# Three small extra reads early in an attention block with adaptive layer norm

## The chip, the cores and the metric

The kernel runs on one core of one Trainium2 chip. A core has five engines that run side by side: TensorE (PE, matrix products), VectorE (DVE), ScalarE (ACT), GpSimd (POOL) and SyncE (SP, which here only issues DMAs). Sixteen DMA engines move data between the chip's main memory and the core's on-chip memory. The metric is the device time of one execution in microseconds (us).

## The reference

It is one attention block of a diffusion transformer. Inputs in bf16: x is 2 x 256 x 1152, c is 2 x 1152, wqkv is 1152 x 3456, wo is 1152 x 1152, w_mod is 1152 x 6912.

```
mod = (silu(c) @ w_mod) in six parts of D: shift, scale, gate, and three that are not used
h   = layernorm(x) * (1 + scale) + shift
q, k, v = h @ wqkv in three parts
p   = softmax(q @ k.T * D**-0.5)          per batch
out = x + gate * ((p @ v) @ wo)
```

## The kernel before

All 512 tokens (2 batches of 256) are held on chip as four tiles of 128 rows, x_sb[0] to x_sb[3]; tiles 0 and 1 are the first batch, 2 and 3 the second. D = 1152 is nine blocks of 128 (k = 0 to 8). The weights come in once, each in pieces.

The start works against the loads. Thirteen matmuls on constants (the fillers) keep TensorE busy until x arrives. Statistics of the layer norm are taken from x tiles 1 and 0, the tiles are centred, turned by TensorE (tp) and copied into xnT. Meanwhile silu(c) is formed from c_sb and, times the pieces of wS (the scale part of w_mod), gives the scale of the first three blocks (scale_A, psS and psSA). VectorE multiplies xnT by the scale into hTs, and TensorE starts on k = h @ wK while the rest is still loading: k_part(0), k_part(1) and k_part(2) over the first batch with row blocks 0, 1 and 2 of wK into six accumulators (acc) and early_half into psE; then x tile 3, x tile 2 and the other row blocks. After that come the shift part (wH), q (wqv pieces 0 to 2), the scores, softmax, v, attention, and the product with wo, gated and added to x.

The order on each engine is written out: every instruction made through vec, sca, ten, spq or gps is recorded, and pin() chains each record in that order. Nearly all DMAs go out on SyncE's queue through spq, in this order: x tiles 1, 0, 3; five pieces of wS (the first three blocks' columns, row pairs 0-2, 2-4, 4-6, 6-8, 8-9); row block 0 of wK in two parts (wK0); row block 1 (wK1); x tile 2; row block 2 (wK2); then further wS and wK pieces, wH, wqv, wG, wO. ScalarE's queue issues c_sb at the start (line 130) and one output piece at the end. These two are called on nc.scalar itself, so pin() does not chain them.

The framework gives each DMA the next of eight completion semaphores in turn, over both queues together. A DMA that takes a semaphore waits until its holder before, eight places earlier, has landed. In the built program of before, the places are: x1, x0, c, x3, then the wS pieces. So wS's fifth piece waits for x1, wK0's parts for x0 and c, wK1 for x3, x2 for wS's first piece, and so on.

Most instructions bear line 74 in the profile, the line of the recording helper, so groups are told by their tiles.

Of the kernel before, what the change touches and what calls it, by code (L numbers as in the profile page):

```python
# [11 lines left out]
BF16 = mybir.dt.bfloat16  # L12
# [4 lines left out]
def kernel(  # L17
# [9 lines left out]
    nc = tc.nc  # L27
    P = 128
    B, N, D = x.shape
# [16 lines left out]
    x_f = x.rearrange("b n d -> (b n) d")  # L46
# [5 lines left out]
    const = ctx.enter_context(tc.tile_pool(name="const", bufs=1))  # L52
# [43 lines left out]
    def tok(b):  # L96
# [5 lines left out]
        out=ident, in_=ident, compare_op=ALU.not_equal, fill=1.0, base=0,  # L102
# [14 lines left out]
        out=pick, in_=pick, compare_op=ALU.is_ge, fill=0.0, base=0,  # L117
# [3 lines left out]
        out=pick, in_=pick, compare_op=ALU.is_ge, fill=0.0, base=NT - 1,  # L121
# [6 lines left out]
    x_sb = act.tile([P, TT, D], BF16)  # L128
    nc.scalar.preload_act_table_set("natural_log_exp_and_others")
    nc.scalar.dma_start(out=c_sb, in_=c.rearrange("b (p k) -> p b k", p=P))  # L130

    wK = wpool.tile([P, KT, D], BF16)
    chunk_cols = [vc * CW for vc in range(NCH)] + [2 * D + vc * CW for vc in range(NCH)]
# [580 lines left out]
```

## Time and profile before

| what | value |
|---|---|
| median of 3 runs | 98.16 us (97.86 to 98.18) |
| profiled execution | 97.95 us, of which 96.2 us span |
| TensorE clock granted, mean | 0.996 |
| DMA moved | 21.31 MB, 222 GB/s over the span |
| x_sb loads, 288 KB each | issue to landing 2.8 / 3.8 / 4.5 us (least, median, most) |
| c_sb load, 4.5 KB | issue to landing 2.9 us |

The span runs from the first to the last instruction; the rest of the execution's time lies around it. A wait in the profile is put down to the releaser that came last. "Landing" is when a DMA's completion semaphore has its full count. A line of the chain of waits gives start, length and the work that held the end up. TensorE's busy time is modelled at the ends of matmuls, so starts are the firmer numbers. SPq and ACTq are the times in which SyncE and ScalarE issue DMAs.

### The profile page before, as it was taken

How to read it: one execution, taken by the hardware profiler on the slowest of the kernel's cores; microseconds unless marked ns; L12 is line 12 of the kernel's file. 1: busy time of each engine (PE TensorE's matmuls, PEld its weight loads, DVE VectorE, ACT ScalarE, POOL GpSimd, SP SyncE). 2: the span in 40 equal slices, each digit the busy share in tenths (PEclk: the TensorE clock that was granted, in tenths of full speed). 3: DMA queues.
4: the chain of work that ended last, by engine and by line, in shares of the span. 5: the costliest groups of instructions: out<-in, count | busy, mean ns of one | idle time of the engine just before them, and what ended most of it. 6: DMA issues, size and time to landing. Idle time of an engine off the chain costs nothing.

```text
span 96.2 us, 1804 instructions
## 1 busy us (share of the span) xinstructions
PE 91.2 (95%) x715; PEld 55.5 (58%) x720; DVE 70.6 (73%) x139; ACT 33.5 (35%) x67; POOL 21.4 (22%) x26
## 2 busy tenths in 40 slices
PE   5998899999999999999999999999999999999970
PEld 1338698454566444444458755665568755665760
DVE  0488589132999999999982999990229577999880
ACT  5297667202560962432231445331115400000010
POOL 6600000710000000000000000008999980007000
PEclk9999999999999999999999999999999999999998
DMA  2999999999999999999999502200000000303221
GB/s 47 303 350 344 348 391 375 396 395 407 395 380 400 383 407 393 373 371 372 383 410 410 220 2 55 50 5 0 0 0 0 7 0 0 123 1 122 98 97 51
DMA packets 19015, 21.31 MB, mean 222 GB/s; under 512 B 2752, under 2 KB 13632, under 8 KB 19008
## 3 DMA queue, kind: packets, MB, share of 16 engines
q1 hardware_dynamic: 18592, 21.16, 61.4%
q10 hardware_dynamic: 416, 0.05, 0.4%
q8 instruction: 5, 0.08, 0.3%
q14 instruction: 2, 0.02, 0.0%
HBM read 19.76 MB, written 1.18 MB: 218 GB/s over the span
## 4 chain that ended last, share of the span: by engine, by line
PE 85%; DMA 9%; DVE 1%; SPq 1%; issue 1%; ACT 0%
PE ps L74 63%; PE acc L74 12%; DMA x_sb<-in_x_dram 4%; DMA wK<-in_wqkv_dram 4%; PE s_ps L74 4%; PE psH L74 2%; PE psE L74 1%; PE tp L74 1%; SPq L74 1%; PE psL L74 1%; DVE xnT L74 0%; PE spread_ps L74 0%; ACT o_sb L74 0%; DVE hTs L74 0%; DVE o_sb L74 0%
## 5 line engine op out<-in xcount | busy, mean ns | idle before, releaser
L74 POOL PARTITION_ALL_REDUCE gate_bc<-gacc x2 | 13.7, 6886 | 45.5 <-DVE gacc L74 45.5
L74 DVE SCALAR_TENSOR_TENSOR gacc<-wG,scT_f,gacc 128x1152 f32<-128x1152 bf16 x16 | 22.7, 1418 | 0.5
L74 PE MATMUL ps<-wqv,hT 128*128 128x384 bf16 x108 | 17.7, 326 | 0.0
L74 PE MATMUL ps<-hT,wqv 128*128 128x512 bf16 x80 | 17.6, 379 | 0.1
L74 PE MATMUL ps<-wO,attnT 128*128 128x384 bf16 (+1 forms) x108 | 17.0, 319 | 0.0
L74 PEld LDWEIGHTS <-attnT 128*128 128x128 bf16 x117 | 11.3, 98 | 6.3
L74 PEld LDWEIGHTS <-hT 128*128 128x128 bf16 x108 | 10.6, 98 | 6.9
L74 PE MATMUL acc<-hTs,wK 128*128 128x128 bf16 (+2 forms) x88 | 13.3, 292 | 0.8 <-DVE hTs L74 0.3
L74 PEld LDWEIGHTS <-wK 128*128 128x128 bf16 x123 | 9.9, 97 | 6.5 <-DMA wK<-in_wqkv_dram 0.7
L74 PEld LDWEIGHTS <-wqv 128*128 128x128 bf16 x81 | 7.8, 97 | 9.6 <-DVE hT L74 0.4
L74 ACT CAST qkT<-ps 128x512 bf16<-128x512 f32 x10 | 5.8, 583 | 10.9 <-PE ps L74 10.9
L74 DVE TENSOR_TENSOR ga<-ps,gate_bc 128x384 f32<-128x384 f32 (+1 forms) x12 | 6.5, 538 | 2.4 <-PE ps L74 2.4
L74 ACT CAST v_sb<-ps 128x384 bf16<-128x384 f32 x10 | 4.7, 476 | 9.8 <-PE ps L74 9.8
L74 DVE TENSOR_TENSOR o_sb<-ga,x_sb 128x384 bf16<-128x384 f32 (+1 forms) x12 | 7.0, 585 | 0.4
L74 DVE TENSOR_TENSOR xnT<-xnT,rstd_bc 128x512 bf16<-128x512 bf16 x9 | 5.5, 685 | 1.8 <-ACT rstd_bc L74 1.8
L74 PE MATMUL junk_ps<-junk_rhs 128*128 128x512 bf16 x13 | 5.7, 627 | 1.1 <-DVE junk_rhs L74 1.1
L74 ACT CAST o_sb<-ps 128x128 bf16<-128x128 f32 x1 | 0.3, 265 | 17.3 <-PE ps L74 17.3
L74 DVE BATCH_NORM_STATS2 stats<-x_sb 128x6 f32<-128x384 bf16 x6 | 3.1, 552 | 2.5 <-DMA x_sb<-in_x_dram 2.5
L74 PE MATMUL ps<-hTs,wK 128*128 128x512 bf16 x19 | 4.7, 378 | 0.1
L74 DVE CAST attnT<-ps 128x512 bf16<-128x512 f32 (+1 forms) x6 | 3.5, 603 | 1.7 <-PE ps L74 1.7
L74 DVE COPY xnT<-tp 128x384 bf16<-128x384 bf16 (+2 forms) x7 | 2.2, 347 | 3.3 <-PE tp L74 3.3
L74 DVE CAST v_sb<-ps 128x384 bf16<-128x384 f32 x2 | 1.1, 558 | 4.6 <-PE ps L74 4.6
(84 smaller groups left out, 91.8 us busy)
## 6 DMA issues: line engine op xcount, KB each, us to landing
wqv<-in_wqkv_dram SPq DMA_DIRECT2D x5, 864.0 KB, 10.1
wG<-in_w_mod_dram SPq DMA_DIRECT2D x3, 864.0 KB, 9.6
wO<-in_wo_dram SPq DMA_DIRECT2D x3, 864.0 KB, 8.5
wH<-in_w_mod_dram SPq DMA_DIRECT2D x4, 576.0 KB, 7.8
wS<-in_w_mod_dram SPq DMA_DIRECT2D x6, 288.0 KB, 6.0
wK<-in_wqkv_dram SPq DMA_DIRECT2D x6, 288.0 KB, 6.2
x_sb<-in_x_dram SPq DMA_DIRECT2D x4, 288.0 KB, 3.8
wqv<-in_wqkv_dram SPq DMA_DIRECT2D x3, 288.0 KB, 9.0
```

Source lines behind the costliest of these rows:

```text
L74: r = fn(*a, **k)
```

## The change

Behind the load of c, ScalarE's queue issues three more reads into a new tile, seen, of 16 partitions. The first takes the first 16 elements (32 bytes) of every eighth row of x tile 2 (16 rows), the second the same of x tile 3. The third takes 32 bytes at column D of every eighth row of wqkv's first 384 rows, 48 rows. Nothing reads seen. The instructions of the other engines keep their order; the three reads take three places in the rotation of the completion semaphores, between x3 and the first piece of wS, so all later DMAs stand three semaphores further.

```diff
     nc.scalar.dma_start(out=c_sb, in_=c.rearrange("b (p k) -> p b k", p=P))
+
+
+    seen = const.tile([16, 5, 16], BF16)
+    for i in range(2):
+        nc.scalar.dma_start(out=seen[:, i, :], in_=x_f[2 * P + i * P : 3 * P + i * P : 8, 0:16])
+    nc.scalar.dma_start(
+        out=seen[:, 2:5, :], in_=wqkv[0 : 3 * P, D : D + 16].rearrange("(k e r) n -> e k r n", k=3, r=8)[:, :, 0, :])
 
     wK = wpool.tile([P, KT, D], BF16)
```

## The prediction

> **What bounds the kernel now.** I read the busy shares first, then the chain that ended last by line, then the same chain in order of time over the first 16 us, then TensorE's timeline, SyncE's timeline and waits, and the DMA rates by stretch.
>
> ```profile
> PE 91.2 (95%) x715; PEld 55.5 (58%) x720; DVE 70.6 (73%) x139; ACT 33.5 (35%) x67; POOL 21.4 (22%) x26
> PE 85%; DMA 9%; DVE 1%; SPq 1%; issue 1%; ACT 0%
> ```
>
> TensorE is the bound, and 85% of the chain lies on it. The 9% of DMA, some 8.7 us, must all lie early. The chain in order of time shows where:
>
> ```profile
> 0.79 0.40 SPq L74
> 1.25 0.41 SPq L74
> 1.71 4.33 DMA x_sb<-in_x_dram
> 6.05 4.32 DMA wK<-in_wqkv_dram
> 10.41 0.83 PE acc L74 x6
> 11.24 0.45 PE tp L74 x8
> 11.69 0.22 PE psE L74 x2
> ```
>
> The reader is to see a chain with two links of DMA. The third load of x (x3, rows 384 to 511, issued at 1.71) lands at 6.03. Only then does SyncE issue the load of wK's second row block (wK1, 256 KB), which lands at 10.37, and TensorE starts on it at 10.41. From there to the end the chain is almost pure TensorE. A change in the first 10 us can therefore move the end by what it moves that start at 10.41, no more in the good direction than the wait there, and one for one in the bad direction.
>
> ```profile
> 9.09 0.81 PE L74 MATMUL acc<-hTs,wK 128*128 128x256 bf16 x6 [0.33 <-DVE hTs L74]
> 9.74 0.38 PE L74 MATMUL psE<-hTs,wK 128*128 128x256 bf16 x2
> 10.41 0.83 PE L74 MATMUL acc<-hTs,wK 128*128 128x256 bf16 x6 [0.29 <-DMA wK<-in_wqkv_dram]
> 11.78 0.83 PE L74 MATMUL acc<-hTs,wK 128*128 128x256 bf16 x6
> ```
>
> The two psE matmuls begin at 9.74. The chain counts such a pair as 0.22 us of work, so TensorE could have gone on at 9.96 and stood until 10.41: 0.45 us (0.29 by the modelled ends). That is the whole prize of an earlier wK1. The wait at 9.09 is for VectorE's hTs, which waited for scale matmuls that follow each other closely from 8.20; an earlier DMA does not shorten it.
>
> ```profile
> 2.17 2.48 SPq L74 DMA_DIRECT2D wS<-in_w_mod_dram  x5
> 4.70 1.68 SPq L74 DMA_DIRECT2D wK<-in_wqkv_dram  x3
> SPq L74 <- DMA x_sb<-in_x_dram: 0.4, 1, 0.4
> ```
>
> SyncE issues about every 0.5 us (5 in 2.48) and its one wait for an x load, 0.4 us, stands ahead of wK1. The rates by stretch, columns as busy time of PE, PEld, DVE, ACT and POOL, then TensorE's clock, the share of the DMA engines and GB/s, say why x3 and wK1 were late:
>
> ```profile
> 2.50:3.50 1.00, 1.00 (x4) 0.31 (x3) 0.00 (x0) 0.00 (x0) 0.86 (x3) 1.00 1.05 341
> 3.50:4.50 1.00, 1.00 (x4) 0.31 (x3) 0.87 (x3) 0.23 (x2) 0.58 (x1) 1.00 0.91 254
> 5.50:8.00 2.50, 2.50 (x33) 1.39 (x31) 2.10 (x6) 2.29 (x7) 0.00 (x0) 1.00 1.09 368
> 8.00:10.00 2.00, 1.67 (x30) 1.42 (x27) 1.68 (x9) 1.60 (x2) 0.00 (x0) 1.00 1.01 333
> ```
>
> The transfers dip to 254 GB/s while x3 comes in and to 333 while wK1 and the last x load (x2, rows 256 to 383) come in; between, they run at 368. In the trace's packets these dips are single packets: most 2304-byte packets take 93 ns, but eight started between 3.63 and 4.07 take 250 to 1027 ns, and six of 2048 or 2304 bytes between 8.03 and 9.47 take 382 to 1289. The extra reads go to just these rows: x's second batch and wqkv's first 384 rows.
>
> **The change part by part.** It removes nothing.
>
> Three more issues on ScalarE's queue, behind that of c. One takes 0.46 us (c's row), so they end near 1.27 + 3 x 0.5 = 2.8. ScalarE's first work waits for c until 3.76. Cost nothing; the cover is 0.9 us of that wait. Without it, the 0.22 us e_sb would come later, then VectorE's silu and ScalarE's copy scT_rep, which itself stands behind act_mean(0) until 5.88.
>
> The bytes themselves: 80 rows of 32 bytes. c's read is the like: its queue shows 272 packets in the stretch 2.0 to 4.5 at a share of 6.1% of 16 engines, 0.15 us per engine. The three reads make 80 data packets and about as many completions as three c's (48): 128/272 x 0.15 = 0.07 us per engine, if nothing in them is slow. They wait behind c's packets (first at 2.5) and pass between x0's and x3's. If each met what x3 met, an engine would stand 0.25 to 1.0 us instead. Lower bound 0.07, upper 1.0; I take 0.1, nearest to c, since c's own packets also read rows nobody had read and took under 0.19.
>
> SyncE's order of waits, the largest part, which the diff does not tell. Each DMA takes the next of eight completion semaphores in turn, and a DMA waits until the one eight places before it has landed. In the built program the three reads take places 4 to 6. So these move forward to an earlier partner's wait: wS's second piece waited for nothing and now waits for x1 (landed 3.56), the third for x0 (4.46), the fourth for c (3.74), the fifth for x3 (6.03; before, for x1). wK0's two parts and wK1 wait for the extra reads, already landed by then. Issue times: second piece 2.65 to 3.58; third 3.16 to 4.48; fourth 3.67 to 4.98; fifth 4.18 to 6.05; wK0's parts 4.69 and 5.17 to 6.55 and 7.05; wK1 6.05 to 7.55; x2 6.61 to 8.05; wK2 7.13 to 8.55. SyncE no longer has wK1 directly behind x3's landing, but three issues later: 1.5 us.
>
> Is that covered? wK1 needed 4.32 us from issue to landing, most of it spent behind earlier transfers. The quickest landing in the trace of a load of that size is x1's, 2.8 us for 288 KB on an empty queue; an output of 288 KB took 2.1. With 7.55 + 2.8 = 10.35 it lands exactly when it did; with 2.1, at 9.65, the queue and not the issue decides and nothing moves; with the full 4.32, at 11.87, 1.5 us late. The engines that are ahead run dry for up to 0.8 us (8.0 us of work begun at 8.6), so the lead that absorbs the next slow packet is gone: if the slow packets of wK1 stay, the engine that meets one ends later by part of that. Between 0 and 1.5 I take 0.25, nearest to x1's row. The scale pieces have less room (kk 8 runs at 8.52, its fifth piece landed at 8.46), but 6.05 + 1.6, the time of a 72 KB output on an empty queue, is 7.65, so the backlog still decides there; only the 0.1 us of extra packets passes through.
>
> By the Trainium skill, DMA: Bandwidth & Descriptors, section Latency and other measured facts, an HBM access takes 0.2 us on average and 2 us at high load. By that rule the slow packets come from load, and reading their rows ahead cures nothing; by the opposite, that they are the first access to something, the sum would be -0.45 + 0.1. No run here shows yet which holds.
>
> What the trace says of it: wK0's parts are the first reads of wqkv and come between 6.2 and 8.0 with no slow packet; the wS pieces first touch w_mod's rows over its whole length with at most 259 ns; and at 11.3 two 768-byte packets take 446 and 341 ns in rows whose neighbours had been read. First contact alone does not make a packet slow here. So I take the slow packets as staying.
>
> Sum: +0.1 (packets) + 0.25 (wK1 issued later) = +0.35 us at 10.41. Behind it TensorE stands only some 0.2 us (at 15.02, for hTs), so nothing gives it back. The profiled execution took 97.95, 96.2 of it span; 98.3 is its sum. The median of the runs shown is 0.21 higher, so against it the forecast is 98.5.
>
> **The rivals.** (1) The reads do cure x3, x2 and wK1. Then x3 lands near 5.3 (x1 and x0 landed 0.9 apart), wK1 is issued at 6.8 and lands by 9.9, and the wait at 10.41 goes: -0.45 + 0.1 = -0.35, 97.8. For it: the slow packets sit in exactly those rows. Against it: wqkv's and w_mod's first reads, and the short lead, since the reads' packets come about 3.3 and x3's from 3.63. It decides once wK1 lands before 10.2. Next late would be wK2 (landed 11.73, used at 11.78), which must come 0.4 earlier too. (2) All is covered: the backlog hides the later issues, 98.2. For it: 2.1 us for an output. Against it: the 0.8 us of dry engines. (3) The reads meet slow packets themselves and hold all engines ahead of x3 and the scale pieces: 0.6 to 1.0 us, of which nothing is covered since kk 8 has 0.06 us to spare: 98.9 to 99.1. Against it: c's packets.
>
> **How the numbers follow.** Forecast case 0.45, 98.5 with its own range 98.2 to 98.9; cure 0.31, 97.7 to 97.9; covered 0.12, 98.1 to 98.3; early hold 0.12. A measurement of this kernel tells 0.3% (0.3 us) from no change. Faster: 0.28 of the cure. Same: 0.03 of the cure, 0.12 covered, 0.15 of the forecast case (its lower third), 0.30. Slower: 0.30 + 0.12 = 0.42. The range has to hold the cure and most of the early hold: 97.6 to 99.0.
>
> **What would show it.** In the profile after: the scale pieces issued in a row with gaps from 3.6 on; SyncE's wait for x_sb ahead of the fifth scale piece; wK1 issued near 7.5 and landing 10.4 to 11; the wait for wK at TensorE larger than 0.29; the rate still dipping between 3.5 and 4.5 and 8 and 10. The prediction is wrong if those dips are gone, if the wait for wK is gone, or if wK1 lands as early as before although issued 1.5 us later.

## The result and the profile after

The changed kernel takes 100.78 us (median of 4 runs, 100.43 to 101.28) against 98.06 us before (97.86 to 98.18, 4 runs): a ratio of 1.0289, 95% interval 1.0243 to 1.0334. It is slower by 2.7 us. The prediction had the direction, but 98.5 us and a range that ended at 99.0. Where an execution below ran at a lower granted clock (0.983, three in all), the medians count it and the ratios do not.

The profiled execution took 100.82 us, 98.9 us of it span. Its busy shares and the chain by engine:

```profile
PE 91.5 (93%) x715; PEld 55.4 (56%) x720; DVE 70.6 (71%) x139; ACT 33.5 (34%) x67; POOL 21.8 (22%) x26
PE 64%; DMA 21%; SPq 10%; issue 1%; ACT 0%; DVE 0%
```

TensorE does the same work in 91.5 us, but its share of the chain fell from 85% to 64%. DMA went from 9% to 21%, and SyncE's issuing (SPq), which had 1%, now has 10%. The chain in order of time (start, length, what held the end up) shows where:

```profile
1.25 3.32 DMA x_sb<-in_x_dram
4.59 0.37 SPq L74
5.00 0.47 SPq L74
5.51 0.47 SPq L74
...
7.92 5.17 DMA wK<-in_wqkv_dram
13.14 0.83 PE acc L74 x6
...
29.69 3.56 SPq L74
33.30 0.85 SPq L74
34.19 12.43 DMA wqv<-in_wqkv_dram
46.66 6.00 PE ps L74 x27
```

Before, the chain from 31 us on has TensorE alone here:

```profile
31.01 10.74 PE ps L74 x49
41.80 8.37 PE ps L74 x38
```

There are two losses, not one. The first is where I looked: x0's landing at 4.57 lets SyncE issue the third scale piece, then seven more follow at about 0.47 us each, and the load at their end, wK2, lets TensorE go on at 13.14. The matmuls that began at 11.78 before begin 1.36 us later. TensorE's starts show how the delay grows from load to load:

```profile
9.62 0.49 PE L74 MATMUL acc<-hTs,wK 128*128 128x256 bf16 x3 [0.33 <-DVE hTs L74]
10.82 0.50 PE L74 MATMUL acc<-hTs,wK 128*128 128x256 bf16 x3 [0.71 <-DMA wK<-in_wqkv_dram]
11.49 0.83 PE L74 MATMUL acc<-hTs,wK 128*128 128x256 bf16 x6
13.14 0.83 PE L74 MATMUL acc<-hTs,wK 128*128 128x256 bf16 x6 [0.15 <-DMA wK<-in_wqkv_dram]
```

The matmuls on wK0 begin 0.53 us late (9.62 for 9.09, behind the scale pieces) and stand again for wK0's second part; those on wK1 are 1.08 us late (11.49 for 10.41) and those on wK2 1.36.

The second loss is paid at 46.66, where TensorE stands for a wqv load. Before, it never waited there. SyncE's long issues of large loads around 30 us are not new: the one that takes 3.56 us took 3.35 before. The waits of TensorE that a DMA or VectorE ended in the changed kernel, a part of the list:

```profile
PE acc L74 <- DMA wK<-in_wqkv_dram: 0.9, 2, 0.7
PE ps L74 <- DMA wqv<-in_wqkv_dram: 0.7, 1, 0.7
PE tp L74 <- DVE xc L74: 0.5, 1, 0.5
PE psS L74 <- DMA wS<-in_w_mod_dram: 0.3, 1, 0.3
```

The DMA rates by stretch (columns as in the prediction's table, the last one GB/s) carry the rest. In the kernel before:

```profile
5.00:10.00 5.00, 4.67 (x60) 3.03 (x58) 4.29 (x15) 4.39 (x9) 0.00 (x0) 1.00 1.05 351
30.00:48.00 18.00, 17.89 (x109) 8.41 (x107) 17.64 (x26) 7.62 (x14) 0.00 (x0) 1.00 1.07 384
```

In the changed kernel:

```profile
5.00:10.00 5.00, 3.81 (x55) 2.56 (x53) 3.91 (x13) 4.66 (x9) 0.00 (x0) 1.00 0.88 258
30.00:48.00 18.00, 17.20 (x117) 8.11 (x116) 15.32 (x25) 7.04 (x13) 0.00 (x0) 1.00 1.08 351
```

Early the engines run dry: share 0.88, 258 GB/s instead of 351. Between 30 and 48 us the DMA engines are as busy as before (1.08 and 1.07), so they have work enough, and yet they move 351 GB/s instead of 384. Three reads of 2.5 KB in all, over by 6 us, cannot do that directly. In the packets of that stretch a row of 768 bytes takes 40.6 ns on average instead of 36.0 and one of 2304 bytes 100.4 instead of 93.6. Nothing in the prediction covers that.

### The profile page after: what moved, and what is told of

Its sections match the earlier page's. It is cut to its first block, busy times and chain, and to the rows that moved or that the text cites. A ratio compares the mean times of both kernels' runs of the same rounds, so it can differ in the third digit from the quotient of the medians.

```text
span 98.9 us, 1807 instructions
## 1 busy us (share of the span) xinstructions
PE 91.5 (93%) x715; PEld 55.4 (56%) x720; DVE 70.6 (71%) x139; ACT 33.5 (34%) x67; POOL 21.8 (22%) x26
## 4 chain that ended last, share of the span: by engine, by line
PE 64%; DMA 21%; SPq 10%; issue 1%; ACT 0%; DVE 0%
PE ps L74 46%; DMA wqv<-in_wqkv_dram 13%; PE acc L74 11%; SPq L74 10%; DMA wK<-in_wqkv_dram 5%; PE s_ps L74 4%; DMA x_sb<-in_x_dram 3%; PE psE L74 1%; PE psM L74 1%; PE psL L74 1%; PE tp L74 1%; PE spread_ps L74 0%; ACT o_sb L74 0%; DVE o_sb L74 0%; PE turn_ps L74 0%
## 5 line engine op out<-in xcount | busy, mean ns | idle before, releaser
L74 PE MATMUL junk_ps<-junk_rhs 128*128 128x512 bf16 x13 | 4.9, 561 | 1.1 <-DVE junk_rhs L74 1.1
L74 ACT ACTIVATE xc<-x_sb 128x1152 bf16<-128x1152 bf16 x3 | 3.5, 1161 | 2.7 <-DMA x_sb<-in_x_dram 2.7
```

Of the source, the lines that this page charges most:

```text
L74: r = fn(*a, **k)
```

## The experiments

The first theory was SyncE's waits (the places among the eight completion semaphores). Its rivals were the rows read and the packets themselves. Each ratio below is against the kernel before, run beside it on the same chip.

**Other rows (e1_other_rows).** The three reads take rows of wo.

```diff
-        nc.scalar.dma_start(out=seen[:, i, :], in_=x_f[2 * P + i * P : 3 * P + i * P : 8, 0:16])
+        nc.scalar.dma_start(out=seen[:, i, :], in_=wo[i * P : (i + 1) * P : 8, 0:16])
-        out=seen[:, 2:5, :], in_=wqkv[0 : 3 * P, D : D + 16].rearrange(...)
+        out=seen[:, 2:5, :], in_=wo[2 * P : 5 * P, 0:16].rearrange(...)
```

> Three extra reads of the same shapes on the same queue and in the same three semaphore places, but of rows of wo, which nothing reads before 43 us. Theory places (the loss is SyncE's later issues, because three of eight completion semaphores are held): as slow as the change, 100.4 to 101.3 us, second scale piece issued near 3.7 and third near 4.6. Rival rows (reading those rows of x and wqkv is what hurts): back to 98.0 to 98.5. If the reads also cure x3, its landing goes back from 5.34 to near 6.0 here; if not, it stays near 5.3.

Measured: 100.58 us, ratio 1.0254 (1.0218 to 1.0291). The rows read do not matter to the loss. x3 landed at 5.98 here and at 5.35 in the change, which alone could look like a cure; but it also landed at 5.66 and at 5.20 in two kernels without any extra read (e4_before_merged and e5_pad160, below), so its landing varies by itself. wK1 and x2 were not cured in the change either: between 9.5 and 11.2 packets of 2048 and 2304 bytes again took up to 1260 ns.

**GpSimd's queue (e2_gpsimd).** The change's reads with nc.gpsimd in place of nc.scalar; SyncE's places are those of before.

> The change's three reads of the same rows, issued on GpSimd's queue, whose DMAs take other semaphores, so that SyncE's loads keep the places and waits of before. Theory places: 98.0 to 98.5 us, scale pieces two to four issued at 2.65, 3.16 and 3.67 without a wait. Rival rows or bytes (the extra packets hold the DMA engines): most of the loss stays, 100 to 101. Rival cure: below 97.9, with no wait of TensorE for wK1.

Measured: 99.07 us, ratio 1.0104 (1.0073 to 1.0135). Most of the loss is gone and SyncE issues the pieces at 2.66, 3.17 and 3.69, but 1% stays, more than the expected 98.0 to 98.5. The profile's rate between 30 and 48 us is still low:

```profile
30.00:48.00 18.00, 17.73 (x115) 8.34 (x114) 15.96 (x25) 7.55 (x14) 0.00 (x0) 1.00 1.08 351
```

That is not all of it. TensorE begins its matmuls on wqv at 33.25 for 32.52 before, 0.73 us late, and loses 0.44 at the wait for wqv by the starts of its matmuls. So in this profile the larger part of what is left was lost early, and what caused that stays open.

**One read (e3_one_read).** Only the read of x tile 2.

> Only the first of the three reads. Theory places: one place is held, so only the fourth scale piece waits for x1 (3.7 instead of 3.67, nothing), the fifth for x0 and wK1 no longer for x3; issues before wK1 are as early as before, so 98.0 to 98.6 us and not a third of the loss. Rival bytes: a third of the loss, near 99.0.

Measured: 98.91 us, ratio 1.0116 (1.0076 to 1.0156). By its time the rival's third of the loss came true; by its trace it did not. The profiled execution (98.4 us) starts its acc matmuls and psM within 0.12 us of before, and loses at TensorE's wait for wqv at 44.4, with 351 GB/s between 30 and 48 us again. So the loss late in the kernel does not go by the number of reads or of places.

**Fewer scale pieces, no reads (e4_before_merged).**

```diff
-    for k0, k1 in PAIRS:
+    for k0, k1 in ((0, 2), (2, 5), (5, 9)):
         load_mod(wS, 1, k0, k1, 0, CA)
```

> No extra reads; the five first scale pieces are made three (row pairs 0-2, 2-5, 5-9), so the loads behind stand two places earlier: wK1 is issued near 4.7 instead of 6.05. Theory places: the DMA engines are kept fuller, TensorE's wait for wK1 shrinks from 0.45, 97.5 to 98.0 us; if the larger last piece lands later, up to 98.4. Rival (the number of places does not matter, the bytes do): 98.0 to 98.3.

Measured: 97.92 us, ratio 1.001 (0.9984 to 1.0036): nothing. wK1 was issued at 4.71 instead of 6.05 and landed at 10.17 instead of 10.37. Here, with the queue already deep, an issue 1.3 us earlier bought a landing 0.2 us earlier. This kernel ran 384 GB/s between 30 and 48 us.

All four kernels with the tile seen ran 351 or 352 GB/s there, the two without it 384. The tile itself does something. The built program has the answer: seen is 160 bytes per partition and lies ahead of the weight tiles. wK begins at byte 39936 of each partition before, which is 156 x 256, and at 40096 after, 160 bytes further; wqv, wS, wH, x_sb and what reuses them move alike. So the second theory was the addresses.

**The shift alone (e5_pad160, e5_pad64).** No read, no tile seen; a constant tile is made 160 or 64 bytes longer.

```diff
-    ones_row = const.tile([1, 512], BF16)
+    ones_row_pad = const.tile([1, 592], BF16)      # 544 for 64 bytes
+    ones_row = ones_row_pad[:, 0:512]
```

> The kernel before with no extra read; one constant tile is 160 bytes per partition longer, so that the weight and x tiles behind it lie 160 bytes higher, as they do in the change (rows start 160 past a multiple of 256 bytes instead of on one). Theory addresses: the transfers run at some 351 GB/s between 30 and 48 us instead of 384, 768-byte packets take 40 ns on average instead of 36, and it costs what the one-read kernel cost, 98.6 to 99.4 us, with a wait of TensorE for wqv near 45 us. Rival places (the tile's size means nothing): 97.7 to 98.2 us and 384 GB/s.

> As the last one, with 64 bytes instead of 160: rows start on a multiple of 64 but not of 256 bytes. If the step that counts is 64 bytes or less: 97.7 to 98.2 us, 384 GB/s between 30 and 48 us. If it is 256 bytes, rows of 768 bytes touch four stretches of 256 instead of three and the rate falls below 375; by the Trainium skill, DMA: Bandwidth & Descriptors, section How a descriptor splits into AXI transactions, that is the case, and the time would lie between 98.2 and 99.2.

Measured: 98.47 us, ratio 1.0091 (1.0065 to 1.0118) with 160 bytes; 98.49 us, 1.0108 (1.006 to 1.0157) with 64. Between 30 and 48 us, with 160 bytes:

```profile
30.00:48.00 18.00, 17.52 (x101) 7.97 (x99) 15.84 (x23) 7.64 (x14) 0.00 (x0) 1.00 1.08 350
```

And with 64 bytes:

```profile
30.00:48.00 18.00, 17.65 (x103) 8.12 (x101) 15.95 (x24) 7.64 (x14) 0.00 (x0) 1.00 1.08 351
```

A padding that nobody writes costs 0.8 us (98.47 lies just below the expected 98.6 to 99.4), about what the kernel with one read lost. Rows of 768 bytes took 40.6 ns with 160 bytes of shift and 41.0 with 64, against 36.0. The Trainium skill, DMA: Bandwidth & Descriptors, section How a descriptor splits into AXI transactions, says that a transfer is cut at multiples of 256 bytes and that a start off such a multiple costs extra. The direction agrees (64 bytes off is as bad as 160, so a multiple of 64 is not enough), though the page words it for bytes that are fetched and here the side that is written was moved. The size does not follow the page's count of beats of 32 bytes: an estimate by it is 26 beats for a row of 768 bytes at 64 and 29 at 160, against 24, so the shift by 160 would cost two and a half times the shift by 64, and the runs show the same cost.

**The change with its addresses kept (e6_aligned).** The tile is [16, 16, 16], 512 bytes, instead of [16, 5, 16].

> The change with its tile made 512 bytes per partition long, so that the tiles behind it start on the same multiples of 256 bytes as before; reads, queue and places are those of the change. Theory addresses plus places: 384 GB/s between 30 and 48 us, no wait for wqv near 45, the second scale piece still issued near 3.7; what is left is the loss of the first 13 us, 98.8 to 99.8 us. If addresses were everything: 97.8 to 98.4. If places were everything: 100.4 to 101.

Measured: 100.7 us, ratio 1.0241 (1.0182 to 1.03), executions 99.53, 100.38, 101.03 and 101.1; the ratio is that of the first two. The rate came back to 384 and there was no wait for wqv, as expected, but the time was above the expected 98.8 to 99.8 in three of four. The two long executions have a mean granted clock of 0.983, the others 1.0 and 0.996, and the profile is of one of the long ones. In its stretches from 10 to 16 us the clock is the column ahead of the DMA share:

```profile
10.00:11.00 1.00, 0.13 (x2) 0.10 (x2) 0.47 (x1) 0.00 (x0) 0.19 (x1) 1.00 1.02 341
11.00:12.00 1.00, 1.00 (x9) 0.69 (x9) 0.00 (x0) 0.00 (x0) 0.00 (x0) 0.99 0.98 256
12.00:13.00 1.00, 1.00 (x9) 0.81 (x8) 0.00 (x0) 0.00 (x0) 0.00 (x0) 0.50 0.93 243
13.00:14.00 1.00, 1.00 (x9) 0.64 (x7) 0.36 (x2) 0.77 (x1) 0.00 (x0) 0.50 0.97 299
14.00:15.00 1.00, 1.00 (x6) 0.71 (x5) 0.82 (x4) 0.97 (x4) 0.00 (x0) 0.50 1.06 370
```

TensorE was nearly idle from 10 to 11 (0.13 us busy), ran on for 1 us at 0.99 and then for 3.4 us at half clock. So the early wait is priced at 1.9 and 2.7 us in the two executions whose clock held (99.53 and 100.38 against 97.64), and at more where it dropped. The change's own executions had 0.995 to 1.0. What sets the drop off is not shown: TensorE's longest stops here were 0.83 and 0.87 us (from 8.7 and from 10.0), and one stop of 1.44 us in e2_gpsimd or 1.12 in e5_pad64 was followed by none.

**The same with fewer scale pieces (e7_aligned_merged).** e6_aligned with e4's three pieces.

> The last one with the first scale pieces in three DMAs (row pairs 0-2, 2-5, 5-9) instead of five, so the loads behind stand two places earlier and wK1 is issued near 6.0 as before. Theory places: most of what was left goes, 98.0 to 98.8 us. Rival (the held places do not matter, the reads' packets hold the engines): as the last one.

Measured: 98.91 us, ratio 1.0148 (1.0111 to 1.0184). wK1 is issued at 5.99, as before, but the last scale piece waits for x0, is issued at 4.52 and lands at 9.42, and TensorE stands 1.0 us for it. Two places given back recover part, a little less than expected (98.0 to 98.8); the waits that remain still hit the scale pieces.

**Packets against places (e8_one_place, e9_three_rows).** Both with the 512-byte tile: one DMA with all 80 rows, or three DMAs of one row each.

```diff
+    nc.scalar.dma_start(     # e8
+        out=seen[:, 0:5, :], in_=wo[0 : 5 * P, 0:16].rearrange("(k e r) n -> e k r n", k=5, r=8)[:, :, 0, :])
```
```diff
+    for i in range(3):       # e9
+        nc.scalar.dma_start(out=seen[0:1, i, :], in_=wo[i * P : i * P + 1, 0:16])
```

> One extra read instead of three, with the same 80 rows of 32 bytes (all of wo) and the tile of 512 bytes that keeps the addresses' multiples: the packets of the change, one place. Theory places: the first wait of a scale piece is the fourth's, for x1, 0.1 us; 97.5 to 98.1 us. Rival packets (80 small reads hold the engines): as the aligned kernel with three reads, 99.5 to 101.

> Three extra reads of one row of 32 bytes each, aligned tile: three places, 3 data packets instead of 80. Theory places: 99.4 to 101.1 us, second scale piece issued near 3.7 and third near 4.5, the DMA rate between 5 and 10 us near 250 instead of 350 GB/s. Rival packets: 97.5 to 98.1.

Measured: 98.08 us, ratio 1.003 (0.9967 to 1.0094) with 80 rows in one place; 99.74 us, 1.0201 (1.0151 to 1.0252) with three rows in three places. The packets cost nothing that can be told within an interval of 1.3% width; the places cost 1.9 us.

**The waits by hand (e10_waits_only, e11_waits_pad).** No read at all. The first kernel only adds the change's three waits; the second also has the 160 bytes. The lines that make load_x and load_mod return their instruction are left out here.

```diff
+    x1, x0, x3 = load_x(1), load_x(0), load_x(3)
+    behind = {2: x1, 4: x0, 8: x3}
     for k0, k1 in PAIRS:
-        load_mod(wS, 1, k0, k1, 0, CA)
+        r = load_mod(wS, 1, k0, k1, 0, CA)
+        if k0 in behind:
+            tc.add_manual_dep(r.ins, behind[k0].ins.name, SYNC_SCHED, reason="only a wait")
```

> No extra read, no extra tile, places as before; only the waits are put in by hand: the second scale piece waits for x1, the third for x0, the fifth for x3, as in the change. Theory places, which is a theory of these waits: 99.2 to 101.1 us with the second piece issued near 3.7, the third near 4.5, the rate between 5 and 10 us near 250 GB/s. Rival (something in the reads themselves): 97.5 to 98.2.

> The last one with the 160 bytes of padding: both causes and not one read. Theory waits plus addresses: the whole loss of the change, 100.0 to 101.3 us, 351 GB/s between 30 and 48 us and a wait of TensorE for wqv near 46 us. If the two shared their loss it would be that of the waits alone.

Measured: 99.49 us, ratio 1.0176 (1.0133 to 1.022) for the waits; 100.53 us, 1.0267 (1.0212 to 1.0322) for waits and padding. The two causes add up: 1.76% and 0.91% are 2.67%, whether added or multiplied. The change itself is 1.0289, inside the interval. In the kernel with the waits alone, SyncE's issues, TensorE's matmuls in wK's stretch and the rates are:

```profile
2.17 3.80 SPq L74 DMA_DIRECT2D wS<-in_w_mod_dram  x5
```
```profile
11.45 0.83 PE L74 MATMUL acc<-hTs,wK 128*128 128x256 bf16 x6 [0.80 <-DMA wK<-in_wqkv_dram]
13.31 0.83 PE L74 MATMUL acc<-hTs,wK 128*128 128x256 bf16 x6 [0.37 <-DMA wK<-in_wqkv_dram]
```
```profile
5.00:10.00 5.00, 3.51 (x55) 2.58 (x54) 3.98 (x13) 4.59 (x9) 0.00 (x0) 1.00 0.93 268
30.00:48.00 18.00, 18.00 (x119) 8.59 (x116) 17.05 (x26) 7.19 (x14) 0.00 (x0) 1.00 1.07 385
```

The five scale pieces now take 3.80 us to issue instead of 2.48, as in the change, and the early rate falls to 268, while the late rate stays at 385. With the padding added it is 351:

```profile
30.00:48.00 18.00, 18.00 (x125) 8.59 (x122) 16.38 (x26) 7.04 (x13) 0.00 (x0) 1.00 1.08 351
```

So by the time the whole loss comes back with not one byte more read. The profile shows only the early half of it: it is of the shortest execution (99.85; the others took 100.39 to 100.73), in which the third wqv chunk landed at 45.84, just as TensorE came to it. The expected wait for wqv near 46 us is not in it, and the three longer executions have no profile.

## Why the prediction was wrong

**SyncE's order of waits: the mechanism right, its price 0.25 us where it was 1.7.** The issue times came out nearly as forecast (second piece 3.75 for 3.58, third 4.59 for 4.48, wK1 6.97 for 7.55 because x3 landed sooner). In the built program the third read stands behind the first scale piece, not ahead of it, so wK1 waits for that piece and x2 for the read; both had landed by 6.0, and nothing hangs on it. The step that failed is "the backlog still decides there", for the scale pieces and then for wK1, which landed at 11.45 instead of 10.37. It was argued from the quickest landing of one load on an empty queue, as if the loads behind did not need the same time. With the queue dry, loads come no faster than SyncE issues them, and the ones in question are small: 192 KB in the 0.83 us between the second and the third scale piece is some 235 GB/s, 96 KB in 0.47 us 209 GB/s. The rows of the changed kernel show it twice, where the second piece comes through and where the two loads of 96 KB behind each other (the fifth piece and wK0's first part) do:

```profile
5.50:6.00 0.50, 0.50 (x4) 0.08 (x3) 0.47 (x2) 0.47 (x4) 0.00 (x0) 1.00 0.68 184
...
8.00:8.50 0.50, 0.47 (x14) 0.36 (x12) 0.27 (x1) 0.26 (x1) 0.00 (x0) 1.00 0.62 162
```

By 13 us the change had moved 3.14 MB where before 3.72 had been moved; at the 353 GB/s that the kernel before had between 5 and 13 us, that is 1.6 us of transfers. It is not idle engines alone. Their share between 5 and 13 us fell from 1.05 to 0.89, 1.3 us for each, but slow packets also became more: from 4.5 to 13 us those of over 250 ns number 32 instead of 10 and take 16.9 us instead of 6.1, 0.7 us more for each engine. In the profiles of the seven kernels without the change's three waits they number 1 to 15, in the six with them 29 to 43, with reads or without (e7_aligned_merged, with a part of the waits, has 24). So the later issues come with more slow packets, which the prediction took as staying the same; why is open. The upper end of this term, 1.5 us, was in the prediction; I took the lower part because x1's row gave a landing just in time for wK1 alone, and the range was built around that. e10_waits_only measures the term: 99.49 - 97.82 = 1.67 us.

**A term that was missing: the tile's place in memory.** The prediction says of the change that it removes nothing and lists only issues, packets and waits. A tile that nobody reads still moves every tile allocated behind it. e5_pad160 measures it at 0.83 us. In the change it is paid at one spot: before, the third wqv chunk landed at 42.32 and TensorE came to it about 1.8 us later; in the change it landed at 46.62, 4.3 us later, while TensorE had been delayed by 1.6. 4.3 - 1.6 - 1.8 leaves 0.9, and TensorE's matmuls there began 0.85 us late. In e5_pad160, without the early loss, the chunk landed at 44.48, 2.2 us later, and TensorE lost 0.55 us there; the rest of the 0.83 is not located. In e11_waits_pad's profile the same rate cost nothing at that spot. So this term goes by how transfers and TensorE fall together, and from 0 to 0.9 us were seen. That transfers far from the change had only 1.8 us to spare could have been read from the loads' landings; I stopped at 15 us, since the chain behind was TensorE's alone.

**The packets.** 0.1 us was taken; e8_one_place has 0.3%, from -0.3 to 0.9, so nothing that can be told.

**The cure did not happen**, as forecast, but for no reason that the prediction could prove: e1_other_rows shows that the rows do not matter to the time, and slow packets came back between 8 and 10 us, where the rate was 265 GB/s. The other dip was gone (363 GB/s from 3.5 to 4.5 us), which the prediction named as a sign of being wrong; but x3 landed even earlier, at 5.20, in e5_pad160, which reads nothing ahead, so the sign says nothing of the reads. By the Trainium skill (DMA: Bandwidth & Descriptors, section Latency and other measured facts), high load makes an access slow. The runs do not bear that out here: the slow packets are most in the kernels whose engines were in part idle, as at 184 GB/s and a share of 0.68 from 5.5 to 6 us. What makes single packets slow in the first 13 us stays open.

**The early hold of the engines** (98.9 to 99.1) came nearest in time, but not by its mechanism: x1 and x0 landed 0.1 to 0.2 us later, as they did in e10_waits_only without a read (3.79 and 4.57), and x3 earlier, so nothing held them.

## What to carry to other kernels

Price a small DMA by what it takes from others: count the places it holds among the completion semaphores, list which load now waits for which landing, and ask whether the queue stays full when SyncE resumes, at so many bytes per issue. A new tile, even an unused one, moves all tiles behind it: compare the start addresses of DMA targets with multiples of 256 bytes before and after, and pad the tile if they left them. And look for the transfer with the least margin in the whole kernel, not only in the stretch of the change, since a lower rate shows up there.

## What the runs showed of the hardware

- Where a load's rows start on chip set its rate: 384 GB/s on multiples of 256 bytes, 350 and 351 at 160 and 64 bytes beyond (30 to 48 us, rows of 768 and 2304 bytes), with all DMA engines equally busy (1.07 and 1.08). Other offsets were not run.
- In one profile (e6_aligned) TensorE's granted clock was 0.50 for 3.4 us, from 1.1 us after a stretch of 2.2 us in which TensorE stood for 1.7. The change stood as long between 5 and 16 us (2.0 us in both) without that, and single stops of 1.0 to 1.4 us in three other profiles (e2_gpsimd, e5_pad64, e7_aligned_merged) did not bring it. The executions with a mean clock of 0.983 took 101.03 and 101.1 us, those without 99.53 and 100.38.
- Single packets of 300 to 1300 ns against 36 to 93 appear above all in the first 13 us of the kernel, whichever rows were read before, and about three times as many when SyncE's issues came late (32 instead of 10 over 250 ns from 4.5 to 13 us). No run here shows their cause.
